# Five of eight pairs of experts: probabilities transposed in 32x32 blocks by VectorE and put in place through DRAM

## The chip, the cores and the metric

The kernel runs on one core of a Trainium2 chip. The metric is the device time of one launch in microseconds, the median of several runs. Engines are named as in the profile: PE is TensorE's matmul and PEld its weight load, DVE is VectorE, ACT is ScalarE, POOL is GpSimd, SP is SyncE, on whose queue all DMAs of this kernel are issued.

## The reference

Three stages follow one another, all in float32, for 4 batches of 448 positions: attention with 12 heads and a soft cap, a gated feed-forward stage with a short convolution, and four experts, each a causal attention of its own, of which two are kept at each position. The change lies in the last one. With `x` from the stage before it, it is:

```python
logits = x @ w_gate                      # (B, S, 4); the two largest are kept, w is their softmax
for e in range(4):
    q, k, v = x @ wq[e], x @ wk[e], x @ wv[e]          # (B, S, 64)
    scores = scale * (q @ k.transpose(0, 2, 1))
    scores = np.where(causal, -1e9, scores)
    a = softmax(scores)                                # (B, S, S)
    ye = a @ v @ wo[e]
    out += (chosen[e] * w[e]) * ye
```

The product `a @ v` sums over keys. TensorE sums over partitions, so the probabilities, which come out of the softmax with queries on the partitions, must be turned so that keys are there.

## The kernel before, in words

All four batches pass through attention first. The feed-forward results of batches 0 to 2 are made in between, left in DRAM (`g_dram`) and read back as the last stage wants them; a convolution with its gate (`conv_gate`, line 878) is done early, ahead of the store, for the first `EARLY_N[b]` of a batch's eight blocks (line 73), and after the read for the others (`prep_g`, line 1007). Then the output weights of the feed-forward stage are folded into those of the experts (`fold_mm`, line 811), and the last stage goes batch by batch.

In the last stage `v_unit` (1133) makes a batch's values and gate logits, in a tile of 4 blocks of 128 keys by 260 columns (the last block half filled), and `proj_unit` (1096) its queries and keys, 8 units of 12 matmuls a batch, which DMAs from SBUF to SBUF (`pl.move`, 1125 to 1131) then bring to the other half of the partitions, 20 for each batch. The experts go in two pairs, `i` = 0 and 1. `scores2` (1191) makes the scores of a pair in seven blocks of queries: three of 128 queries for each of the two experts, with 128, 256 and 384 keys, and one that holds the last 64 queries of both, with 448 keys. VectorE masks them and finds their maximum, ScalarE takes the exponential into SBUF, and `norm2` (1222) scales them by one over the sum and the gate's weight.

`tr2` (1241) turns them: for each expert two units of four TensorE transposes of 128x128 into a PSUM bank (banks 5 and 6 in turn, `TB`), and from there two copies, of 448 and of 64 columns, into SBUF (`PTT`, eight tiles of 512). So a pair has 16 transposes and 8 copies. `pv2` (1264) multiplies by the values, key block after key block, with the two experts side by side in the two halves of TensorE's columns, and `wo_unit` (1287), for the last batch `wo_first` and `wo_rest`, make the output, six blocks a batch.

The order of the work is a written-out list. The program makes every operation (`Plan.add`, line 238) without issuing it; `ORDER` (line 78) then says in which order the operations are issued, and so the order on each engine and on SP's queue. `SWAP` (line 178) lists the operations that go to the other of VectorE and ScalarE than the code says. `Plan.pages` (218) only serves to find out which operations depend on which. Each engine works through its own part of the list in order. The tail of the program is in the order of `TAIL` (line 193), before the list rearranges it.

Of the kernel before, what the change touches and what calls it, by code (L numbers as in the profile page):

```python
# [19 lines left out]
E = 4  # L20
# [21 lines left out]
HALF_END = 1  # L42
# [30 lines left out]
EARLY_N = (0, 4, 4, 0)  # L73
TR_E = (0, 0)
# [115 lines left out]
T_ORDER = ("q0", "q1", "tr0", "tr1", "pv0", "tr2", "tr3", "pv1", "wo")  # L190
T_LAST = ("q0", "q1")
T_REST = 12
TAIL = ("2tr0", "2tr1", "2pv0", "3q0", "2tr2", "2tr3", "3q1", "2pv1", "3tr0", "3tr1", "2wo0", "2wo1", "3pv0",
        "2wo2", "2wo3", "2wo4", "2wo5", "3tr2", "3tr3", "3woA", "3pv1", "3woB")


# [1232 lines left out]
```

## Time and profile before

| | |
|---|---|
| median of 3 runs | 530.38 us (530.14 to 531.41) |
| the profiled execution | 530.21 us |
| its span, first to last instruction | 528.5 us |
| TensorE matmul, busy | 520.6 us (99%), 3312 instructions |
| VectorE, busy | 451.8 us (85%) |
| ScalarE, busy | 364.9 us (69%) |
| DMA | 63.84 MB, mean 121 GB/s |

The profile is of one execution. Attention takes the time to about 230 us, the folding to about 362, and the last stage the rest. Busy time of TensorE includes the modelled ends of its pipelined matmuls. In groups of instructions a line is that of a helper for most operations: 380 issues matmuls, 384 transposes, 314 ScalarE's operations, 322 VectorE's, 389 DMAs. `ps` is PSUM, `fm` the float32 tile in SBUF and `rm` the one for TensorE's fast float32 format.

### The profile page before, as it was taken

How to read it: one execution, taken by the hardware profiler on the slowest of the kernel's cores; microseconds unless marked ns; L12 is line 12 of the kernel's file. 1: busy time of each engine (PE TensorE's matmuls, PEld its weight loads, DVE VectorE, ACT ScalarE, POOL GpSimd, SP SyncE). 2: the span in 40 equal slices, each digit the busy share in tenths (PEclk: the TensorE clock that was granted, in tenths of full speed). 3: DMA queues.
4: the chain of work that ended last, by engine and by line, in shares of the span. 5: the costliest groups of instructions: out<-in, count | busy, mean ns of one | idle time of the engine just before them, and what ended most of it. 6: DMA issues, size and time to landing. Idle time of an engine off the chain costs nothing.

```text
span 528.5 us, 9365 instructions
## 1 busy us (share of the span) xinstructions
PE 520.6 (99%) x3312; PEld 413.5 (78%) x3312; DVE 451.8 (85%) x1083; ACT 364.9 (69%) x659; POOL 9.8 (2%) x64
## 2 busy tenths in 40 slices
PE   9999999999999999999999999999999999999997
PEld 6445587555665855869999999999978988999886
DVE  6999999999788888899869999999978998947662
ACT  7999949999896869944224556356857884736662
POOL 4000000000000000000000002000000000000000
PEclk9999999999999999999999999999999999999999
DMA  6635534342322422244564541155334325404514
GB/s 212 194 125 191 166 134 153 122 127 73 117 92 69 131 69 87 61 142 142 180 213 147 160 138 38 53 160 145 84 95 122 92 82 154 102 9 102 141 52 158
DMA packets 42543, 63.84 MB, mean 121 GB/s; under 512 B 7424, under 2 KB 31360, under 8 KB 42496
## 3 DMA queue, kind: packets, MB, share of 16 engines
q1 hardware_dynamic: 42496, 63.24, 39.5%
q8 instruction: 26, 0.43, 0.3%
q14 instruction: 21, 0.17, 0.1%
HBM read 40.94 MB, written 12.85 MB: 102 GB/s over the span
## 4 chain that ended last, share of the span: by engine, by line
PE 90%; ACT 4%; DVE 2%; DMA 2%; SPq 1%; issue 1%
PE ps L380 87%; ACT fm L314 3%; PE ps L384 2%; DVE fm L322 1%; DVE rm L322 1%; SPq L389 1%; DMA fm<-w_in 1%; DMA fm<-kq 1%; ACT rm L314 1%; DMA rm<-rm 0%; DVE ps L322 0%
## 5 line engine op out<-in xcount | busy, mean ns | idle before, releaser
L380 PE MATMUL ps<-rm 128*128 128x448 f32 (+5 forms) x2316 | 399.4, 350 | 3.2 <-ACT fm L314 2.3
L380 PEld LDWEIGHTS ps<-rm 128*128 128x128 f32 (+1 forms) x2316 | 353.1, 187 | 47.4 <-ACT fm L314 9.8
L314 ACT ACTIVATE fm<-fm 128x448 f32<-128x448 f32 (+6 forms) x217 | 162.1, 773 | 35.8 <-DVE fm L322 21.8
L322 DVE SCALAR_TENSOR_TENSOR fm<-fm 128x448 f32<-128x448 f32 (+4 forms) x240 | 148.2, 631 | 8.6 <-ACT fm L314 5.7
L314 ACT ACTIVATE fm<-ps,fm 128x896 f32<-128x896 f32 (+5 forms) x142 | 110.0, 794 | 31.8 <-DVE fm L349 12.6
L380 PE MATMUL ps<-fm 128*64 128x448 f32 (+9 forms) x868 | 114.7, 470 | 1.7 <-DVE fm L578 1.1
L380 PEld LDWEIGHTS ps<-fm 128*64 128x64 f32 (+4 forms) x868 | 46.1, 135 | 63.1 <-issue 49.1
L322 DVE TENSOR_TENSOR rm<-fm,rm 128x448 fp32r<-128x448 f32 (+3 forms) x154 | 87.1, 583 | 4.7 <-ACT rm L314 3.2
L314 ACT ACTIVATE fm<-ps 128x448 f32<-128x448 f32 (+4 forms) x111 | 49.3, 468 | 49.6 <-PE ps L380 34.3
L322 DVE TENSOR_TENSOR fm<-fm 64x448 f32<-64x448 f32 (+6 forms) x112 | 60.9, 550 | 5.0 <-ACT fm L314 2.7
L322 DVE TENSOR_SCALAR fm<-fm 128x256 f32<-128x256 f32 (+8 forms) x143 | 43.1, 315 | 10.7 <-ACT fm L314 6.8
L314 ACT ACTIVATE rm<-fm 128x448 fp32r<-128x448 f32 (+5 forms) x77 | 39.6, 543 | 12.1 <-DVE fm L322 7.1
L314 ACT ACTIVATE rm<-ps 128x386 fp32r<-128x386 f32 (+3 forms) x46 | 19.9, 438 | 29.8 <-PE ps L380 28.7
L322 DVE COPY fm<-ps 128x448 f32<-128x448 f32 (+5 forms) x47 | 20.1, 434 | 12.6 <-PE ps L380 7.7
L322 DVE CAST rm<-fm 128x448 fp32r<-128x448 f32 (+4 forms) x85 | 29.7, 367 | 1.1 <-PE ps L380 0.3
L322 DVE TENSOR_TENSOR rm<-ps,rm 128x386 fp32r<-128x386 f32 (+1 forms) x32 | 18.7, 586 | 4.5 <-ACT rm L314 4.2
L322 DVE TENSOR_TENSOR fm<-fm,ps 128x448 f32<-128x448 f32 (+1 forms) x30 | 16.4, 568 | 5.3 <-PE ps L380 3.9
L349 DVE CUSTOM_DVE_ANT_0 ps<-ps,fm 128x256 f32<-128x256 f32 (+1 forms) x32 | 11.4, 364 | 7.0 <-PE ps L380 6.0
L384 PE MATMUL ps<-fm 128*128 128x128 f32 x128 | 17.2, 272 | 0.0
L384 PEld LDWEIGHTS ps<-fm 128*128 128x128 f32 x128 | 15.0, 140 | 1.2
L322 DVE TENSOR_REDUCE fm<-ps 128x1 f32<-128x384 f32 (+1 forms) x24 | 13.8, 576 | 0.4
L314 ACT ACTIVATION_READ_ACCUMULATOR fm<-ps,fm 128x1 f32 x56 | 11.0, 196 | 0.0
(24 smaller groups left out, 64.4 us busy)
## 6 DMA issues: line engine op xcount, KB each, us to landing
g_dram<-fm SPq DMA_DIRECT2D x32, 224.0 KB, 2.3
fm<-g_dram SPq DMA_DIRECT2D x32, 224.0 KB, 2.9
fm<-w_in SPq DMA_DIRECT2D x24, 256.0 KB, 2.7
fm<-woT SPq DMA_DIRECT2D x16, 384.0 KB, 3.3
fm<-kq SPq DMA_DIRECT2D x23, 256.0 KB, 3.3
out<-fm SPq DMA_DIRECT2D x23, 224.0 KB, 2.3
fm<-v SPq DMA_DIRECT2D x24, 192.0 KB, 2.7
fm<-kq SPq DMA_DIRECT2D x23, 192.0 KB, 3.2
```

The costliest lines, as they stand in the source:

```text
L314: return self.add("act", cost, [lambda: self.nc.scalar.activation(out, in_, func, **kw)], [out] + more, [in_] + ptr)
L322: return self.add("dve", cost, [lambda: f(out, *ins, **kw)], [out], aps)
L349: self.add("dve", cost, [lambda: self.nc.vector.tensor_tensor_reduce(x, x, mask, -1.0, 3.0e38, OP.add, OP.min, least)], [x, least], [x, mask])
L380: self.nc.tensor.matmul(out, a, b, start=start, stop=stop, **kw))
L384: calls = [lambda o=o, i=i, d=d: self.nc.tensor.transpose(o, i, d) for o, i, d in parts]
L389: self.add("dma", 470.0, [lambda: self.nc.sync.dma_start(out, in_)], outs, ins, size=size, **kw)
```

## The change

For five of the eight pairs (all but both of batch 0 and the second of batch 3, `BY_PE`) the transposes on TensorE go. The exponential writes the probabilities of a pair into one tile of 128 x 2048 columns, arranged as four parts `m` of 16 blocks of 32 columns; VectorE turns each part in place, 32x32 block by block (four instructions of 128x512). Two stores bring the tile to DRAM (`p_dram`) and four loads bring it back, so that partition 4x+m holds key 32m+x of each block of 128 keys. The values of batches 1 to 3 are put in the same order of keys by one store and one load (`spread_v`). In `pv2` a product is cut in two: the whole query blocks, and the shared block of 64 queries.

The other three pairs are turned as before, with four PSUM banks (`QB`) that they share with the scores. The shared block of scores now goes through the exponential with 512 columns, the last 64 of them at -1e30, which VectorE writes into the four banks at first and again after each turn of batch 0 (`hide_rest`). `EARLY_N` goes from 4 to 8 for batch 2. The identity for the transposes is made later, the half-filled key block lies in the lower partitions instead of the upper ones, and a branch that was not taken goes (`HALF_END`). `ORDER` and `SWAP` are new throughout; there are 2497 operations instead of 2489.

```diff
-EARLY_N = (0, 4, 4, 0)
+EARLY_N = (0, 4, 8, 0)
...
-TAIL = ("2tr0", "2tr1", "2pv0", "3q0", "2tr2", "2tr3", "3q1", "2pv1", "3tr0", "3tr1", "2wo0", "2wo1", "3pv0",
-        "2wo2", "2wo3", "2wo4", "2wo5", "3tr2", "3tr3", "3woA", "3pv1", "3woB")
+TAIL = ("2pv0", "2pv1", "3q0", "3q1", "2wo0", "2wo1", "2wo2", "2wo3", "2wo4", "2wo5", "3pv0", "3woA", "3pv1", "3woB")
+P2_AT = ((0, 1, 2), (5, 2, 1))
+BY_PE = ((0, 0), (0, 1), (3, 1))
+P2_S = 12
+P2_R = 32 * (P2_S + NT)
...
+    def hide_rest():
+
+        for t in QB.bufs:
+            x = t[:, S:]
+            pl.add("dve", 190.0, [lambda x=x: nc.vector.memset(x, -1.0e30)], [x], [])
+
-    QB, TB = Ring([bank(3), bank(4)]), Ring([bank(5), bank(6)])
+    QB = Ring([bank(i) for i in range(3, 7)])
...
-        pl.act(P2[i][k], ps[:, :n], AF.Exp, bias=mx, scale=-1.0 if fused else 1.0, accum_out=RS2[i][:, 0, k:k + 1])
+        x = ps if shared else ps[:, :n]
+        x = x if (b, i) in BY_PE else x.rearrange("p (n m x) -> p n m x", m=4, x=32)
+        pl.act(P2[i][k], x, AF.Exp, bias=mx, scale=-1.0 if fused else 1.0, accum_out=RS2[i][:, 0, k:k + 1])
...
+    def spread_v(b):
+        x, to = V2F
+        pl.store(v_dram[b], x, keys_out=[("v", b)])
+        pl.load(to, v_dram[b].rearrange("(m k) x -> k m x", m=4), keys_in=[("v", b)])
+        V2[b, "spread"] = V2T.bufs[1]
...
+    def turn(b, i):
+        if (b, i) in BY_PE:
+            return turn_by_pe(b, i)
+        t, PT[i] = P2[i][NS], PTT.next()
+        for m in range(4):
+            x = t[:, P2_R * m:P2_R * m + P2_R]
+            pl.dve("transpose", x, x)
+            if m % 2:
+                c = slice(P2_R * (m - 1), P2_R * (m + 1))
+                pl.store(p_dram[2 * b + i][:, c], t[:, c], keys_out=[("p", b, i, m // 2)])
+        for a in range(4):
+            to = PT[i][:, P2_R * a:P2_R * a + P2_R]
+            src = p_dram[2 * b + i, 32 * a:32 * a + 32].rearrange("k (m x) -> (k m) x", m=4)
+            pl.dma(to, src, sb_out=to, size=128 * P2_R * 4, keys_in=[("p", b, i, 0), ("p", b, i, 1)])
...
     def pv2(b, i):
         ps = R1 if i else bank(1)
         parts = []
+        by_pe = (b, i) in BY_PE
+        vt = V2[b] if by_pe else V2[b, "spread"]
+        u = None if by_pe else PT[i].rearrange("p (a n x) -> p n a x", a=4, x=32)
         for c in range(NT):
...
+                if c < NK:
+                    at_, sj, sc = P2_AT[h]
+                    n = at_ + (sj + sc) * c
+                    o = ps[a, 128 * c:128 * NK].rearrange("p (j a x) -> p j a x", a=4, x=32)
+                    parts.append((o, y, u[:, n:n + sj * (NK - 1 - c) + 1:sj], c == 0, False))
+            for h, (a, _) in enumerate(sides):
+                e = 2 * i + h
+                y = vt[:, c, D * e:D * e + D]
+                parts.append((cut(ps[a, 128 * NK:S], 2), y, u[:, P2_S + c, 2 * h:2 * h + 2], False, c == NK))
         pl.mm(parts)
```

`turn` is the last unit of a pair's scores; `turn_by_pe` is `tr2` for the whole pair with banks of `QB`, followed by `hide_rest` for batch 0.

The numbers in `ORDER` count the operations as the program makes them, so the last ones can be told from the end (2496): 21 of `wo_rest` (from 2476), 3 of `pv2` for pair (3,1), 5 of `wo_first`, 3 of `pv2` for (3,0) (2465 to 2467, TensorE first), 18 of batch 2's output (2447 to 2464, TensorE's every third), 12 of `turn_by_pe` for (3,1) (2435 to 2446), 10 of its `norm2`, 24 of its scores (2401 to 2424), 10 of `turn` for (3,0) (2391 to 2400: two transposes, a store, two transposes, a store, four loads), 10 of its `norm2`, 24 of its scores (2357 to 2380), 2 of `spread_v` for batch 3 (2355, 2356), and 3 each of `pv2` for (2,1) (from 2352) and (2,0) (from 2349). The stretch of the new list around that turn:

```diff
+2298 2382 2383 2384 2274 2390 2385 2272 2100 2386 2388 2387 2389 2394 2395 2335 2391 2337 2343 2344 2392 2134 2350
+2275 2352 2351 2338 2345 2346 2336 2401 2353 2354 2404 2348 2402 2407 2403 2405 2347 2406 2411 2408 2447 2412 2330
+2332 2135 2409 2410 2414 2453 2415 2396 2334 2413 2417 2418 2393 2448 2356 2419 2421 2422 2423 2454 2416 2131 2399
+2450 2456 2451 2459 2397 2420 2424 2400 2425 2462 2426 2398 2427 2434 2431 2430 2429 2449 2428 2432 2433 2438 2455
+2444 2445 2435 2439 2457 2436 2441 2442 2446 2440 2463 2443 2465 2437 2473 2452 2474 2466 2467 2472 2470 2468 2471
```

## Rows read from the trace of the kernel before

**Rows 1.** The page, part 1: busy us (share of the span) and count of each engine.

```profile
PE 520.6 (99%) x3312; PEld 413.5 (78%) x3312; DVE 451.8 (85%) x1083; ACT 364.9 (69%) x659; POOL 9.8 (2%) x64
```

**Rows 2.** Stretches: length, busy us of PE, PEld, DVE, ACT, POOL, clock, DMA share, GB/s.

```profile
0.00:57.00 57.00, 52.95 (x396) 28.58 (x396) 51.44 (x129) 52.97 (x59) 5.92 (x51) 1.00 0.54 173
57.00:362.00 305.00, 305.00 (x1890) 239.36 (x1891) 273.14 (x545) 205.32 (x308) 3.62 (x11) 1.00 0.39 121
362.00:528.00 166.00, 162.64 (x1030) 145.57 (x1028) 127.17 (x412) 106.61 (x294) 0.22 (x2) 1.00 0.37 103
```

**Rows 3.** The waits of TensorE's matmuls: us in total, times, longest.

```profile
PE ps L380 <- ACT fm L314: 2.8, 6, 0.9
PE ps L380 <- DVE fm L578: 1.1, 1, 1.1
```

**Rows 4.** The chain of waits by line, then in time: start, us, what.

```profile
by line: PE ps L380 87.5%; ACT fm L314 3.2%; PE ps L384 2.3%; DVE fm L322 1.3%; DVE rm L322 1.0%; SPq L389 0.9%; issue 0.8%; DMA fm<-w_in 0.7%; DMA fm<-kq 0.6%; ACT rm L314 0.5%; DMA rm<-rm 0.5%; DVE ps L322 0.1%
...
56.96 317.03 PE ps L380 x1972
374.00 0.87 PE ps L384 x8
...
424.50 0.44 PE ps L384 x4
424.94 2.45 PE ps L380 x12
...
497.98 2.38 DMA rm<-rm
...
500.41 0.73 PE ps L380 x4
```

**Rows 5.** TensorE's groups by shape, whole run: busy us, mean ns.

```profile
L384 PE MATMUL ps<-fm 128*128 128x128 f32 x128 | 17.2, 272 | 0.0
...
L380 PE MATMUL ps<-fm 128*64 128x64 f32 x32 | 2.3, 220 | 0.0
```

**Rows 6.** TensorE in time: two pairs' products with the values (start, us, what).

```profile
388.91 3.68 PE L380 MATMUL ps<-fm 128*64 128x448 f32 x32
```

**Rows 7.** VectorE's and ScalarE's groups by shape, whole run: busy us, mean ns.

```profile
L322 DVE SCALAR_TENSOR_TENSOR fm<-fm 128x448 f32<-128x448 f32 x128 | 81.7, 649 | 5.5 <-ACT fm L314 4.2
...
L314 ACT ACTIVATE fm<-ps 128x448 f32<-128x448 f32 x80 | 42.2, 541 | 37.9 <-PE ps L380 25.2 <-DVE fm L322 7.1 <-PE ps L384 4.5
...
L322 DVE SCALAR_TENSOR_TENSOR fm<-fm 128x896 f32<-128x896 f32 x24 | 27.5, 1146 | 1.5 <-ACT fm L314 1.5
...
L322 DVE TENSOR_SCALAR fm<-fm 128x448 f32<-128x448 f32 x13 | 5.8, 449 | 2.6 <-ACT fm L314 1.9 <-DMA fm<-g_dram 0.7
...
L314 ACT ACTIVATE fm<-ps 128x64 f32<-128x64 f32 x16 | 3.5, 220 | 0.0
...
L322 DVE COPY fm<-ps 128x64 f32<-128x64 f32 x16 | 3.4, 217 | 2.1 <-ACT fm L314 2.1
```

**Rows 8.** SP's queue in time: start, us, what it issues.

```profile
448.17 33.69 SPq L389 DMA_DIRECT2D rm<-rm  x20
...
499.25 0.46 SPq L389 DMA_DIRECT2D rm<-rm  x1
```

**Rows 9.** SP's own waits: us in total, times, longest.

```profile
SPq L389 <- DVE fm L322: 166.7, 61, 9.2
```

**Rows 10.** DMA: queue 1 (packets, MB, share); issues: KB each, us to landing.

```profile
q1 hardware_dynamic: 42496, 63.24, 39.5%
...
g_dram<-fm SPq DMA_DIRECT2D x32, 224.0 KB, 2.3
fm<-g_dram SPq DMA_DIRECT2D x32, 224.0 KB, 2.9
fm<-w_in SPq DMA_DIRECT2D x24, 256.0 KB, 2.7
...
fm<-wo SPq DMA_DIRECT2D x2, 384.0 KB, 3.8
```

More of the change, by code (lines that the diff above doesn't have):

```diff
@@ L41 @@
 MERGE = ()
-HALF_END = 1
 P_3 = 10
@@ L72 @@
 PR_L = 110.0
-EARLY_N = (0, 4, 4, 0)
-TR_E = (0, 0)
+EARLY_N = (0, 4, 8, 0)
 V_N = (4, 2, 2, 2)
@@ L229, in pages @@
                 runs = [(lo, hi + step * (n - 1)) for lo, hi in runs]
-        halves = {min(p // 64, 1) for p in (first, first + dims[0][1] - 1)}
+        quarters = range(first // 32, (first + dims[0][1] - 1) // 32 + 1)
         for lo, hi in runs:
@@ L234, in pages @@
                 whole = lo <= page * self.PAGE and hi >= (page + 1) * self.PAGE
-                for h in halves:
-                    yield (ap.tensor.name, h, page), whole and dims[0][1] >= 64
+                for h in quarters:
+                    yield (ap.tensor.name, h, page), whole and dims[0][1] >= 32
     def add(self, eng, cost, calls, outs, ins, keys_out=(), keys_in=(), size=0, modes=None):
@@ L471, in chain_kernel @@
     g_dram = tc.dram_tile([B, 128, NF, S], F32, name="g_dram")
+    v_dram = tc.dram_tile([B, 128, NT * NV], F32, name="v_dram")
+    p_dram = tc.dram_tile([2 * B, 128, 4 * P2_R], F32, name="p_dram")
     def at(pos, kind=None):
@@ L496, in decode @@
         pl.stt(m.bitcast(I32), lo, 29, c, OP.logical_shift_right, OP.bitwise_or)
-    ident, one_0, low_row = fm.take(128), fm.take(96), fm.take(1)
+    ident_at = fm.at
+    one_0, low_row = fm.take(96), fm.take(1)
     cw = fm.take(NF * 3)
@@ L591, in chain_kernel @@
     at(-50)
-    pl.add("pool", 500.0, [lambda: make_identity(nc, ident)], [ident], [])
     one_r = [cut(t, 3) for t in (one_0, one_1)]
@@ L974, in chain_kernel @@
     OTT = fm.ring(3, S)
-    V2T = Ring([cut(t, NT) for t in fm.ring(2, NT * NV).bufs])
+    V2F = fm.ring(2, NT * NV).bufs
+    V2T = Ring([cut(t, NT) for t in V2F])
     gt, ge = (fm.take(NT * E * E, gate_at + n).rearrange("p (k a b) -> p k a b", k=NT, a=E) for n in (0, 64))
@@ L983, in chain_kernel @@
     MXT = fm.ring(4, 1)
-    P2T = fm.ring(2, 2 * 768 + S)
-    PTT = fm.ring(8, 512)
+    P2T, PTT = fm.ring(2, 4 * P2_R), fm.ring(2, 4 * P2_R)
     GX, VS = cut(fm.take(NF * KR), NF), fm.take(NV)
@@ L1072, in chain_kernel @@
             base=0, channel_multiplier=0)
+    ident = fm.take(128, ident_at)
     def late_loads(pos):
         at(pos)
+        pl.add("pool", 500.0, [lambda: make_identity(nc, ident)], [ident], [])
         for t in QZT.bufs + QLT.bufs:
             for a, c in ((lo64, slice(SG - 64, SG)), (hi64, slice(SG - 128, SG - 64))):
-                pl.act(t[a, c], ident[a, :64], AF.Copy, scale=0.0)
+                pl.act(t[a, c], tri[a, :64], AF.Copy, scale=0.0)
         for t in QPT.bufs:
@@ L1082, in late_loads @@
         for t in V2T.bufs:
-            pl.pool("memset", t[:64, NK, :E * D], 0.0, cost=400.0)
-        pl.pool("memset", VS[:64, :E * D], 0.0, cost=400.0)
+            pl.pool("memset", t[64:, NK, :E * D], 0.0, cost=400.0)
+        pl.pool("memset", VS[64:, :E * D], 0.0, cost=400.0)
         for i in range(2):
@@ L1135, in v_unit @@
         if t == 0 and not part:
-            V2[b] = V2T.next()
+            V2[b] = V2T.bufs[not b]
         if not part:
@@ L1154, in v_unit @@
             for x, a in both:
-                pl.pick(0, x[64:], ps[a, :NV])
+                pl.pick(0, x[:64], ps[a, :NV])
             for x, a in both:
-                pl.pick(1, x[:64, E * D:], ps[a, E * D:NV])
+                pl.pick(1, x[64:, E * D:], ps[a, E * D:NV])
     def gate(b):
@@ L1211, in scores2 @@
             t = P2T.next()
-            at_ = [0, 128, 384, 768, 896, 1152, 1536, 1536 + S]
-            P2[i] = [t[:, at_[x]:at_[x + 1]] for x in range(NS)]
+            u = t.rearrange("p (m n x) -> p n m x", m=4, x=32)
+            at_ = [0, 128, 384, 768, 896, 1152, 1536, 4 * P2_R]
+            P2[i] = [t[:, at_[x]:at_[x + 1]] for x in range(NS)] if (b, i) in BY_PE else [u[:, at_ + sj * x:at_ + sj * x + sc * x + 1:sc] for at_, sj, sc in P2_AT for x in range(NK)]
+            P2[i] += [t] if (b, i) in BY_PE else [u[:, P2_S:], t]
             RS2[i] = RST.next()
@@ L1239, in chain_kernel @@
     TR_SH = ((0, 1), (3, 2))
-    def tr2(b, e, k):
-        i, h = divmod(e, 2)
-        if not h and not k:
-            for x in range(2):
-                PT[2 * i + x] = [PTT.next(), PTT.next()]
-        ps = TB.next()
-        at_, sh, to = TR_AT[h][k]
-        parts = []
-        for (c, j), n in zip(TR_C[k], at_):
-            parts.append((ps[:, n:n + 128], P2[i][NK * h + j][:, 128 * c:128 * c + 128], ident))
-        c = TR_SH[h][k]
-        kk = slice(128 * c, 128 * c + 128) if c < NK else slice(S - 128, S)
-        out = ps[:, sh[0]:sh[0] + 128]
-        if sh[1] - sh[0] != 64:
-            n = min(sh[0], 128)
-            out = cut(ps[:, n:n + 384], 2)[:, :, sh[0] - n:sh[0] - n + 64]
-        parts.append((out, P2[i][NS - 1][:, kk], ident))
-        pl.transposes(parts)
-        own = slice(64 * h, 64 * h + S)
-        either(TR_E[k], PT[e][k][:, :S], ps[:, own])
-        other = sh[1 - h]
-        either(TR_E[1 - k], PT[e ^ 1][k][:, to:to + 64], ps[:, other:other + 64])
+    def spread_v(b):
[3 more added lines that the diff above has]
+        V2[b, "spread"] = V2T.bufs[1]
@@ new lines, in turn_by_pe @@
+    def turn_by_pe(b, i):
+        t = PTT.next()
+        PT[i] = [[t[:, 1024 * h + 512 * k:1024 * h + 512 * k + 512] for k in range(2)] for h in range(2)]
+        for h in range(2):
+            for k in range(2):
+                ps = QB.next()
+                at_, sh, to = TR_AT[h][k]
+                parts = []
+                for (c, j), n in zip(TR_C[k], at_):
+                    parts.append((ps[:, n:n + 128], P2[i][NK * h + j][:, 128 * c:128 * c + 128], ident))
+                c = TR_SH[h][k]
+                out = ps[:, sh[0]:sh[0] + 128]
+                if sh[1] - sh[0] != 64:
+                    n = min(sh[0], 128)
+                    out = cut(ps[:, n:n + 384], 2)[:, :, sh[0] - n:sh[0] - n + 64]
+                parts.append((out, P2[i][NS - 1][:, 128 * c:128 * c + 128], ident))
+                pl.transposes(parts)
+                own = slice(64 * h, 64 * h + S)
+                either(0, PT[i][h][k][:, :S], ps[:, own])
+                other = sh[1 - h]
+                either(0, PT[i][1 - h][k][:, to:to + 64], ps[:, other:other + 64])
+        if (b, i) != (B - 1, 1):
+            hide_rest()
@@ L1266, in pv2 @@
         parts = []
+        by_pe = (b, i) in BY_PE
+        vt = V2[b] if by_pe else V2[b, "spread"]
+        u = None if by_pe else PT[i].rearrange("p (a n x) -> p n a x", a=4, x=32)
         for c in range(NT):
+            if by_pe:
+                for h, (a, _) in enumerate(sides):
+                    e = 2 * i + h
+                    rhs = PT[i][h][c in (1, 2)][:, PT_C[h][c]]
+                    parts.append((ps[a, 128 * c:S], vt[:, c, D * e:D * e + D], rhs, c == 0, c == NK))
+                continue
             for h, (a, _) in enumerate(sides):
                 e = 2 * i + h
-                rhs = PT[e][c in (1, 2)][:, PT_C[h][c]]
-                parts.append((ps[a, 128 * c:S], V2[b][:, c, D * e:D * e + D], rhs, c == 0, c == NK))
+                y = vt[:, c, D * e:D * e + D]
[4 more added lines that the diff above has]
+                    parts.append((o, y, u[:, n:n + sj * (NK - 1 - c) + 1:sj], c == 0, False))
+            for h, (a, _) in enumerate(sides):
+                e = 2 * i + h
+                y = vt[:, c, D * e:D * e + D]
+                parts.append((cut(ps[a, 128 * NK:S], 2), y, u[:, P2_S + c, 2 * h:2 * h + 2], False, c == NK))
         pl.mm(parts)
@@ L1303, in wo_rest @@
                 pl.mm(wo_parts(b, m, wop[m], (1,)))
-            elif not HALF_END:
-                wop.append(TB.next())
-                pl.mm(wo_parts(b, m, wop[m], (0, 1)))
             else:
@@ L1310, in wo_rest @@
                 for k in range(2):
-                    c, ps, ot = slice(n * k, n * k + n), TB.next()[:, :n], PTT.next()[:, :n]
+                    c, ps, ot = slice(n * k, n * k + n), QB.next()[:, :n], GT.next()[:, :n]
                     pl.mm([(ps, x, y[:, c], *z) for _, x, y, *z in wo_parts(b, m, ps, (0, 1))])
@@ L1315, in wo_rest @@
                 continue
-            wo_out(b, m, wop[m], PTT.next()[:, :S])
+            wo_out(b, m, wop[m], GT.next())
     def unit(cost, f, *args, lag=0.0):
@@ L1335, in t_parts @@
         for i in range(2):
-            parts[f"q{i}"] = [unit(0.3, scores2, b, i, k) for k in range(NS)] + [unit(0.0, norm2, b, i)]
+            parts[f"q{i}"] = [unit(0.3, scores2, b, i, k) for k in range(NS)] + [unit(0.0, norm2, b, i), unit(0.5, turn, b, i)]
             parts[f"pv{i}"] = [unit(1.9, pv2, b, i)]
-        for e in range(E):
-            parts[f"tr{e}"] = [unit(0.5, tr2, b, e, k) for k in range(2)]
         return parts
@@ L1355, in chain_kernel @@
             late_loads(pos)
+            hide_rest()
         pos = merge(proj_units(b), with_prep(b + 1, t), pos)
+        if b:
+            at(pos, "spread%d" % b)
+            spread_v(b)
     b = B - 1
@@ L1361, in chain_kernel @@
         p, k = (t3 if n[0] == "3" else t2), n[1:]
+        if n == "3q0":
+            at(pos, "spread%d" % b)
+            spread_v(b)
         if k in p:
```

2 lines of the change are left out of this document (1 added, 1 removed), and 211 rows, old and new, of tables (ORDER, SWAP).

## The prediction

> **What bounds the kernel now.** I read the page's summary first. TensorE is busy for 520.6 of 528.5 us [rows 1]. Then the stretches: the granted clock is 1.00 in each, so the upper of its two levels; between 57 and 362 us TensorE is busy for 305.00 of 305 us, and between 362 us and the end for 162.64 of 166; VectorE is at 273.14/305 = 90% and 127.17/166 = 77% there, ScalarE lower, the DMA engines at 0.39 and 0.37 [rows 2]. The two longest waits of TensorE's matmuls sum to 3.9 us [rows 3], and the chain of waits runs through TensorE for 317 us without a break [rows 4]. So nothing hides TensorE's work: an instruction less there is time less, as long as what replaces it is never waited for.
>
> **What leaves TensorE.** A pair of experts has 16 transposes (two experts, two units, four each); 8 pairs make the 128 of the trace [rows 5]. The chain shows 8 of them in 0.87 us and 4 in 0.44, so 0.109 us each, with the matmul behind them at its usual pace (12 in 2.45 us) [rows 4]: switching costs nothing beside them. The same line holds 2.3% of the chain, 12.2 us for the 112 transposes on it, again 0.109. Five of eight pairs go: 80 x 0.109 = **8.7 us less**. The other end is the group's busy time, 17.2 x 5/8 = 10.8 us [rows 5], but its ends are modelled and overlap the next instruction; I keep 8.7.
>
> **What comes onto TensorE.** The products with the values had 448 + 320 + 192 + 64 = 1024 columns for each expert; now they have 384 + 256 + 128 and four pieces of 64, 1024 again. Two pairs take 32 instructions in 3.68 us [rows 6]: each float32 product runs as two instructions, with two experts side by side. There are three more products an expert, so 3 x 2 x 5 = 30 more such side-by-side instructions. If only columns count they cost 0. At most each costs what the 64-column form shows, 2.3 us / 16 = 0.144, less its columns' 0.058 (64 of the 4096 columns in 3.68 us), or 0.086 x 30 = 2.6 us [rows 5, 6]; but that again is mostly a modelled end. A gain is excluded, the columns being the same. Nearest is the dense run itself, whose 16 steps follow one another without an idle time in the view, so near the lower end: an eighth of the way, **0.35 us more**.
>
> **VectorE.** It gets 20 transposes of 128x512, an operation that the trace doesn't show. From below it is at the pace of the scalar operation, 0.449 us for 448 columns, so about 0.5; from above 1.15 us, an operation of 896 columns. The one-pass float32 operations take 0.649 us for 448 columns and 1.146 for 896, so 0.72 for 512 [rows 7]; a transpose is one such pass, so I take that: 14.4 us. The 12 memsets of 64 PSUM columns, at the 0.217 us of a 64-column copy out of PSUM, add 2.6. Gone are 20 copies of 448 columns out of PSUM (0.541 us, mostly ScalarE) and 20 of 64 (0.22, half on each engine): 13 us of ScalarE, 2.2 of VectorE [rows 7]. Four conv gates of batch 2 move from after 362 us to before it (EARLY_N 4 to 8), each four three-operand instructions of 0.649 on VectorE: 10.4 us. So after 362 us VectorE has 127 + 14.8 - 10.4 = 131 of about 158 us, 83%; before, 273 + 10.4 = 284 of 305, 93%. It stays below TensorE in both, and all of this is hidden under TensorE at nothing; without that cover it would cost up to the 14.8 us of its sum. The wider shared block (512 columns for 448) adds 64 x 0.84 ns = 0.05 us to each of eight exponentials, hidden too. The later identity, the moved padding and the branch that goes fall to POOL, 2% busy [rows 1], or to nobody: nothing. The finer pages of the planner issue no instruction.
>
> **DMA and its queue.** Five pairs bring 2 stores of 512 KB and 4 loads of 256 KB each, three batches one store and one load of 520 KB: 36 transfers, 13.7 MB. All go on SP's queue, at 0.46 us an issue [rows 8], 17 us of a queue that waited 166.7 us for one VectorE line alone [rows 9]. Queue 1 moved 63.24 MB in 39.5% of the span, so 303 GB/s when busy [rows 10]; 13.7 MB is 45 us, and the last stretch goes from 0.37 to about 0.64. Hidden, as long as nobody waits for a landing.
>
> **The tightest place** is pair (3,0), in the tail. Counted in the new list, the operations of TensorE between the last VectorE transpose (2392) and that pair's product with the values (2465) are the product of pair (2,1), 3.68/2 = 1.84 us [rows 6]; fifteen score matmuls of pair (3,1), 4416 columns, 2.0; 36 output matmuls of batch 2 at 0.204, 7.35; sixteen transposes, 1.74 [rows 4]: 12.9 us of cover. The round trip under it: four transposes 2.9; a 512 KB store, from 2.3 (224 KB) to 4.5 (the loads' 2.9 at 224 KB and 3.8 at 384 KB, extended), taken at 3.4; five issues in front of the last load, 1.9; its landing, 2.7 to 3.8, taken at 3.0 [rows 8, 10]. Together 11.2, at best 8.9 (transposes of 0.5 us) and at worst 14.8 (of 1.15): a slack of 1.7, or a wait of 1.9 us. For the other four pairs a batch's projections (8 units of 12 matmuls at 0.204, 20 us) stand in between. For new waits in all I take 0.8 us, between 0 and 1.9.
>
> The Trainium skill, "DMA: Bandwidth & Descriptors", section "Anatomy of one DMA — SWDGE (gpsimd) path", gives 2.0 us and bytes over 436 GB/s for another issue path: 3.2 us for the store, 2.6 for the load. The trace agrees about the fixed part (2.3 and 2.9 us for 224 KB), so by it nothing would be waited for, and the sum would be 0.8 us less, 522.0.
>
> **Sum.** The profiled execution took 530.21 us, of which 528.5 is its span: 530.21 - 8.7 + 0.35 + 0.8 = 522.65. The median of the runs is 0.17 above that execution: **522.8 us**.
>
> **The rivals.**
> *Part is given back.* The new order leaves TensorE waiting for landings at two or three places (the product of pair (2,1), the values of batch 3, pair (3,0)). Each late landing costs at most 2.3 to 2.9 us [rows 10]; one to two of them beside the above give 525 to 528.5. For it: the short waits [rows 3] belong to the old order, and the list is wholly new. Against it: the cover counted above.
> *No gain.* What leaves TensorE comes back as waits, because the transpose through VectorE takes 11 us from end to end where TensorE takes 16 x 0.109 = 1.7; 1.7 us uncovered in each of five pairs is 8.4, and the time 531. The Trainium skill says so in "VectorE: DVE Perf Modes", section "Rules for kernel authors": a 128x128 transpose belongs on TensorE where its result may go to PSUM, VectorE turning blocks of 32x32 only. The trace speaks for it only in that the copies out of PSUM were nearly free here; against it, TensorE is the one engine that is full [rows 2].
> *Slower: SP's queue.* It issues in order. A load that waits for its pair's store holds every transfer behind it for the store's landing, about 3.4 us. Behind it stand the moves that put queries and keys of the next batch in place: 20 of them between 448 and 482 us, and at 497.98 one for which TensorE's next matmul waited [rows 4, 8]. Six holds (four pairs, two V reorders) fall among those moves. With no slack, three cost 10.2 us: 530.4 - 8.35 + 10.2 = 532.3. It decides from 10 us of holds that reach TensorE. Against it: the queue is mostly idle, and the moves come in bursts.
> *More.* Only the first 57 us leave TensorE idle, for 4.05 us [rows 2]. If the new list wins that back too, the time is 518.6.
>
> **How the numbers follow.** A measurement of this kernel can tell about 0.3% from no change, 1.6 us: faster is below 528.8, slower above 532.0. Chances: gain kept (520.5 to 524.5) 0.62; part given back 0.16; more 0.06; no gain 0.07; slower 0.09. Faster sums to 0.84. The range goes from 518.5, the first stage's idle time won back (the 10.8 us of the other end would give 520.5, inside it), to 529, where the second case ends; it leaves out the last two cases and half of "more", 0.19.
>
> **What would show it.** Right: 48 transposes on TensorE at 0.109 us, 20 on VectorE near 0.72 us, TensorE still busy for 305 us of the middle, its matmuls' waits below 6 us in all, ScalarE some 13 us shorter. Wrong: waits of TensorE for DMA of the turned tiles or for the moves, VectorE transposes above 1.5 us, idle stretches of TensorE between 180 and 362 us behind conv gates, or matmuls of 64 columns that take more than 0.1 us each pair.

## The result, and the profile after

The changed kernel takes 524.45 us (median of 4 runs, 523.81 to 526.76) against 530.79 for the kernel before on the same chip: a ratio of 0.989 (95% interval 0.9855 to 0.9922), 6.3 us less. A second set of runs on another chip gave 525.3 against 530.65, 0.990 (0.9887 to 0.9915). The forecast was 522.8, in a range of 518.5 to 529.0: inside the range, 1.7 us below the result. The profiled execution took 524.19 us, 6.0 less than that of before.

First the page's line of engines, part 1, then the stretches (length, busy us of PE, PEld, DVE, ACT, POOL, clock, DMA share, GB/s), both of the kernel after; they answer to [rows 1, 2].

```profile
PE 511.1 (98%) x3292; PEld 405.8 (78%) x3292; DVE 451.6 (86%) x1075; ACT 366.2 (70%) x659; POOL 9.3 (2%) x64
```

```profile
57.00:362.00 305.00, 305.00 (x1894) 239.19 (x1891) 275.56 (x547) 218.85 (x336) 4.04 (x15) 1.00 0.39 119
362.00:522.00 160.00, 153.78 (x1010) 138.95 (x1008) 124.70 (x399) 94.55 (x269) 0.00 (x0) 1.00 0.63 193
...
400.00:440.00 40.00, 38.77 (x274) 35.70 (x273) 37.25 (x100) 30.83 (x81) 0.00 (x0) 1.00 0.76 237
...
480.00:500.00 20.00, 18.80 (x137) 15.89 (x136) 14.94 (x55) 10.61 (x34) 0.00 (x0) 1.00 0.90 282
```

The last stage is shorter, but TensorE, idle there for 166 - 162.64 = 3.4 us before, is now idle for 6.2; 2.6 and 2.7 us of these lie behind its last matmul. VectorE reads 124.70 of 160, 78%, as an average; the third line is the stretch that matters, 37.25 of 40 us, 93%, with the DMA engines at 0.76. The waits of TensorE's matmuls in the kernel after (us in total, times, longest) show where the idle time is; they answer to [rows 3]:

```profile
PE ps L381 <- ACT fm L315: 3.8, 7, 1.1
PE ps L381 <- DVE fm L582: 1.1, 1, 1.1
PE ps L381 <- DMA fm<-p_dram: 0.9, 1, 0.9
PE ps L381 <- DVE rm L323: 0.8, 1, 0.8
PE ps L381 <- DMA rm<-rm: 0.7, 2, 0.4
PE ps L381 <- ACT rm L315: 0.6, 1, 0.6
```

They sum to 7.9 us; the same view of before summed to 4.3 (the two rows of [rows 3] and one of 0.4). From 362 us on it is 3.3 for 0.4; the 0.8 for VectorE's line 323 is new too, but lies in the first 57 us. Two are new in kind: the turned probabilities' loads, and the moves. TensorE in time shows them (start, us, what, and in brackets the idle time before it). The second line is the product of pair (1,1) with the values, held 0.93 us; the third, held 0.30, is TensorE's next work behind it.

```profile
432.06 1.98 PE L381 MATMUL ps<-fm 128*64 128x384 f32 x28
434.97 1.98 PE L381 MATMUL ps<-fm 128*64 128x384 f32 x28 [0.93 <-DMA fm<-p_dram]
437.25 4.09 PE L381 MATMUL ps<-rm 128*128 128x256 f32 x21 [0.30 <-DMA rm<-rm]
...
507.96 3.71 PE L381 MATMUL ps<-fm 128*64 128x384 f32 x44
```

The groups by shape of the kernel after (busy us, mean ns) show the operations that stayed and those that came, and its DMA view (KB each, us to landing) the transfers:

```profile
L323 DVE STREAM_TRANSPOSE fm<-fm 128x512 f32<-128x512 f32 x20 | 13.2, 692 | 0.2
...
L385 PE MATMUL ps<-fm 128*128 128x128 f32 x48 | 5.7, 272 | 0.0
...
L1197 DVE MEMSET ps<- 128x64 f32 x12 | 1.2, 112 | 0.2
```

```profile
q1 hardware_dynamic: 47680, 76.92, 47.5%
...
p_dram<-fm SPq DMA_DIRECT2D x10, 512.0 KB, 3.5
fm<-p_dram SPq DMA_DIRECT2D x20, 256.0 KB, 4.3
...
rm<-rm SPq DMA_DIRECT2D x32, 128.0 KB, 3.0
```

The loads land in 4.3 us. The moves, untouched by the change, land in 3.0 us; in the run without the new transfers, below, the same row says 2.3.

### The profile page after: what moved, and what is told of

Read it like the earlier page. It is cut to its first block, busy times and chain, and to the rows that moved or that the text cites. A ratio compares the mean times of both kernels' runs of the same rounds, so it can differ in the third digit from the quotient of the medians.

```text
span 522.5 us, 9375 instructions
## 1 busy us (share of the span) xinstructions
PE 511.1 (98%) x3292; PEld 405.8 (78%) x3292; DVE 451.6 (86%) x1075; ACT 366.2 (70%) x659; POOL 9.3 (2%) x64
## 4 chain that ended last, share of the span: by engine, by line
PE 91%; DVE 2%; DMA 2%; ACT 2%; SPq 1%; issue 1%; ACTq 0%
PE ps L381 90%; ACT fm L315 2%; DVE fm L323 1%; DMA rm<-rm 1%; SPq L390 1%; PE ps L385 1%; DVE rm L323 1%; DMA fm<-kq 1%; ACT rm L315 0%; ACTq L315 0%
## 5 line engine op out<-in xcount | busy, mean ns | idle before, releaser
L315 ACT ACTIVATE fm<-fm 128x448 f32<-128x448 f32 (+7 forms) x231 | 167.2, 758 | 42.5 <-DVE fm L323 32.9
L315 ACT ACTIVATE fm<-ps,fm 128x896 f32<-128x896 f32 (+4 forms) x142 | 110.2, 795 | 27.5 <-DVE fm L323 12.9
L381 PE MATMUL ps<-fm 128*64 128x448 f32 (+10 forms) x928 | 114.8, 450 | 2.9 <-DVE fm L582 1.1
L323 DVE TENSOR_TENSOR rm<-fm,rm 128x448 fp32r<-128x448 f32 (+4 forms) x154 | 86.6, 584 | 3.4 <-ACT rm L315 2.3
L315 ACT ACTIVATE fm<-ps 128x448 f32<-128x448 f32 (+5 forms) x87 | 39.4, 471 | 36.1 <-PE ps L381 26.5
L315 ACT ACTIVATE rm<-fm 128x448 fp32r<-128x448 f32 (+4 forms) x83 | 43.3, 546 | 18.3 <-DVE fm L323 14.1
L323 DVE TENSOR_SCALAR fm<-fm 128x256 int32<-128x256 int32 (+12 forms) x129 | 38.5, 313 | 6.0 <-DMA fm<-g_dram 1.6
L323 DVE CAST rm<-fm 128x384 fp32r<-128x384 f32 (+5 forms) x79 | 27.4, 360 | 1.2 <-DMA fm<-kq 0.8
L323 DVE COPY fm<-ps 128x448 f32<-128x448 f32 (+4 forms) x32 | 16.0, 512 | 14.0 <-PE ps L381 12.0
L323 DVE STREAM_TRANSPOSE fm<-fm 128x512 f32<-128x512 f32 x20 | 13.2, 692 | 0.2
```

The lines of the kernel that those rows point to most:

```text
L315: return self.add("act", cost, [lambda: self.nc.scalar.activation(out, in_, func, **kw)], [out] + more, [in_] + ptr)
L323: return self.add("dve", cost, [lambda: f(out, *ins, **kw)], [out], aps)
L381: self.nc.tensor.matmul(out, a, b, start=start, stop=stop, **kw))
```

## The experiments

**The change once more**, with no edit, beside the three runs on record with it.

> The changed kernel itself, beside the three others: the time to compare them with. 524.4 us again by every theory (523.8 to 525).

525.3 us (524.55 to 526.0), the 0.990 given above; this is what the next runs on the kernel after are held against. The later ones come from other chips, where the kernel before took 530.58 to 530.82.

**What the transposes on TensorE were worth.** Four runs. The first adds 16 transposes ahead of each of the five changed products, 80 in all, to the kernel after.

```diff
         pl.mm(parts)
+        if not by_pe:
+            pl.ops[-1].calls[:0] = [lambda: nc.tensor.transpose(ps[:, :128], ident, ident)] * 16
```

> The changed kernel, with 16 transposes of the identity put on TensorE ahead of each of the five new products with the values (their result is overwritten). Theory (TensorE is full, so each of its instructions is paid): 80 x 0.109 = 8.7 us more than the changed kernel, 533.1 us (532 to 534). Rival (the last stage is now set by waits, of which TensorE's idle time there shows 3.5 us): these 3.5 us take up part of it, 529 to 530.

It took 530.42 us, a ratio of 0.9995 (0.9986 to 1.0004) to before: 5.1 us more than the change beside it (525.3), not 8.7; neither figure came, the rival's is the nearer. With the transposes back, the new order takes as long as the old. TensorE's waits for the turned probabilities are gone from its view and their sum falls to 5.5 us: part of the added work lies where TensorE waited.

The second takes the 80 transposes out of the kernel before and leaves everything else, its order too.

```diff
         pl.transposes(parts)
+        if (b, i) not in ((0, 0), (0, 1), (3, 1)):
+            pl.ops[-1].calls.clear()
```

> The kernel before, in its old order, with the 80 TensorE transposes of the same five pairs left out and the copies out of PSUM kept (the five pairs compute other values). Theory (the whole gain is TensorE's time): 530.8 - 8.7 = 522.1 us (521.5 to 522.8), which is 2.3 less than the changed kernel. Rival (the gain of the changed kernel comes from the new list and the earlier conv gates, and the transposes were partly hidden): 526 or more.

It took 527.37 us, 0.9939 (0.9926 to 0.9953): only 3.3 us of the 8.7, and the rival's figure. The third also leaves out the 40 copies out of PSUM that follow these transposes.

```diff
         either(TR_E[k], PT[e][k][:, :S], ps[:, own])
+        if (b, i) not in ((0, 0), (0, 1), (3, 1)):
+            pl.ops[-1].calls.clear()
         other = sh[1 - h]
         either(TR_E[1 - k], PT[e ^ 1][k][:, to:to + 64], ps[:, other:other + 64])
+        if (b, i) not in ((0, 0), (0, 1), (3, 1)):
+            pl.ops[-1].calls.clear()
```

> The kernel before without the 80 TensorE transposes of the five pairs and also without their 40 copies out of PSUM (13 us of ScalarE, about 2 of VectorE; the five pairs compute other values). Leaving out the transposes alone gave 527.4. First theory (the copies, in ScalarE's order, are what TensorE then waits for): 530.65 - 8.7 = 522 us. Second theory (VectorE at 37 of 40 us, and the softmax that TensorE now reaches earlier): 527.4, no more gained; in between, 524 to 526, if both.

526.11 us, 0.9912 (0.9899 to 0.9925): another 1.3 us, so the copies are a part of what is missing, but a small one. In TensorE's timeline of this run three waits for ScalarE are left behind 480 us, 1.85 us in all:

```profile
484.09 8.16 PE L380 MATMUL ps<-rm 128*128 128x384 f32 x41 [0.71 <-ACT fm L314]
...
497.77 1.83 PE L380 MATMUL ps<-rm 128*128 128x384 f32 x8 [0.91 <-ACT fm L314]
499.83 5.73 PE L380 MATMUL ps<-rm 128*128 128x128 f32 x27 [0.23 <-ACT fm L314]
```

The fourth run starts again from the second, with the copies in, and makes room on VectorE and ScalarE: it also leaves out the steps of the last batch's convolution gates.

```diff
+        for o in pl.ops:
+            if str(o.kind).startswith("prep_g3") and o.eng != "dma":
+                o.calls.clear()
         pl.issue()
```

> The kernel before without the 80 transposes (527.4 us) and, on top, without the 36 VectorE and 28 ScalarE steps of the last batch's convolution gates (22 us and 15 us of work after 362 us): the last batch's gates are left out, its transposes are left out. Theory: after 362 us the two engines beside TensorE are as full as TensorE, and that is why leaving the transposes out gave 3.3 us and not 8.7; with room on both the rest comes back: 522 us. Rival: it is chains in the order of the steps (a softmax's row sums, a copy that frees a bank), which stay as long when the engines are emptier: 526 us or more.

525.63 us, 0.9907 (0.9893 to 0.992): 1.7 us by the medians, 2.3 by the spans of the two profiled executions, between the theory's 522 and the rival's 526, near the rival, and the stretches say why. First two of the kernel before, then three of the kernel without the transposes, then three without the gates too:

```profile
400.00:440.00 40.00, 39.95 (x269) 36.26 (x268) 37.13 (x109) 30.17 (x79) 0.00 (x0) 1.00 0.36 98
...
480.00:500.00 20.00, 20.00 (x128) 17.24 (x128) 15.45 (x64) 13.85 (x42) 0.00 (x0) 1.00 0.46 122
```

```profile
400.00:440.00 40.00, 38.38 (x243) 34.06 (x242) 37.69 (x112) 30.71 (x82) 0.00 (x0) 1.00 0.38 105
440.00:480.00 40.00, 39.51 (x232) 37.17 (x232) 28.64 (x93) 21.53 (x58) 0.00 (x0) 1.00 0.35 89
480.00:500.00 20.00, 17.58 (x104) 14.35 (x103) 15.55 (x66) 15.02 (x47) 0.00 (x0) 1.00 0.47 130
```

```profile
400.00:440.00 40.00, 39.77 (x250) 35.57 (x251) 27.17 (x93) 21.46 (x62) 0.00 (x0) 1.00 0.39 109
440.00:480.00 40.00, 40.00 (x236) 37.75 (x235) 21.43 (x80) 18.25 (x53) 0.00 (x0) 1.00 0.36 91
480.00:500.00 20.00, 17.36 (x102) 13.85 (x101) 15.12 (x65) 15.48 (x49) 0.00 (x0) 1.00 0.41 116
```

Between 400 and 440 us VectorE was already 93% busy before the change. Without the transposes TensorE arrives early and waits there; with 10 us less work on VectorE and 9 on ScalarE in the stretch it is full again (38.38 to 39.77, then 40.00). That is the theory of two full engines, for some 2 us; the run leaves out work and the order's steps together, so which of the two engines it was stays open. Between 480 and 500 us this theory fails: TensorE loses 2.4 us of 20 without its transposes and gets none of it back when the gates go. TensorE's timeline of the kernel without the transposes names what it waits for:

```profile
485.20 8.14 PE L380 MATMUL ps<-rm 128*128 128x384 f32 x41 [1.36 <-ACT fm L314]
...
495.62 1.95 PE L380 MATMUL ps<-fm 128*64 128x448 f32 x16 [0.40 <-ACT fm L314]
...
498.88 1.83 PE L380 MATMUL ps<-rm 128*128 128x384 f32 x8 [0.65 <-ACT fm L314]
500.95 3.31 PE L380 MATMUL ps<-rm 128*128 128x128 f32 x15 [0.24 <-ACT fm L314]
```

Four waits for ScalarE, 2.65 us, and without the gates the same four sum to 2.64; without the copies, which ScalarE mostly makes, 1.85 are left. Neither engine is full there (15 of 20 us). Before, 31 transposes stood in these 20 us, 3.4 us at 0.109. My reading, which no run tries alone, is that they filled the time while the scores and softmax of the last batch went from engine to engine. So in the old order, by this reading, about 2.3 us of the 8.7 were hidden by full engines between 400 and 480 us, and 2.65 by such a chain after 480. With the 2.9 us by which the span fell that is 7.9; 0.8 stays unassigned.

**What the replacement costs.** The kernel after without the 30 transfers of the probabilities, whose products then use stale values:

```diff
                 pl.store(p_dram[2 * b + i][:, c], t[:, c], keys_out=[("p", b, i, m // 2)])
+                pl.ops[-1].calls.clear()
...
             pl.dma(to, src, sb_out=to, size=128 * P2_R * 4, keys_in=[("p", b, i, 0), ("p", b, i, 1)])
+            pl.ops[-1].calls.clear()
```

> The changed kernel without the 30 transfers that bring the turned probabilities through DRAM (the products read what batch 0 left in the tile, so the five pairs compute other values; VectorE's transposes stay). Theory (what was given back are waits for landings, its own and those of the moves beside them: four waits, 1.8 us): 524.4 - 1.8 = 522.6 us, and the moves land in 2.3 us again instead of 3.0. Rival (the new list has ScalarE late in two places, 1.7 us, and landings cost nothing): 524.4, the same as the changed kernel. Second rival (every wait of the last stage hangs on the transfers): 524.4 - 3.5 = 520.9.

523.28 us, 0.987 (0.9851 to 0.9889): 2.0 us less than the change beside it, about the 1.8 of the theory. The share of the DMA engines between 400 and 440 us falls from 0.76 to 0.49, and the moves land in

```profile
rm<-rm SPq DMA_DIRECT2D x32, 128.0 KB, 2.3
```

But TensorE's waits from 362 us on only fall from 3.3 to 2.8 us, and 2.1 of these are now for the moves. So the 2.0 us are the price of the transfers as a whole, with their issues and traffic; the run doesn't give the price of the late landings alone.

Then the same without VectorE's 20 transposes too:

```diff
             pl.dve("transpose", x, x)
+            pl.ops[-1].calls.clear()
```

> The changed kernel without the 30 transfers and without the 20 VectorE transposes (the five pairs compute other values). Leaving out the transfers alone gave 523.3. First theory (VectorE's 13.2 us are hidden): 523.3 again. Second theory (VectorE shares the bound of the last stage): 1 to 3 us less, 520.5 to 522.5, with TensorE's waits for ScalarE and VectorE shorter.

522.74 us, 0.9844 (0.9831 to 0.9856): 0.5 us less again by the medians, 1.4 by the two ratios, whose intervals just overlap. It lies between the two theories (523.3, and 520.5 to 522.5), so VectorE's 13.2 us cost some 0.5 to 1.4 us, hardly clear of the scatter. It is also a floor: with nothing in place of TensorE's 80 transposes the new order gives 522.7, and what is left are waits for the moves (2.6 us), ScalarE (2.4) and VectorE (2.5), of which 3.2 lie after 362 us. How much more VectorE could take was asked by running ten of the transposes three times over:

```diff
             pl.dve("transpose", x, x)
             if m % 2:
+                pl.ops[-1].calls *= 3
+            if m % 2:
```

> The changed kernel with two of the four VectorE transposes of each pair done three times (the same values): 20 more, 20 x 0.692 = 13.8 us of VectorE. First theory (VectorE is hidden under TensorE at nothing): 525.0 us, as the changed kernel. Second theory (VectorE and TensorE are both full where pairs (1,0) and (1,1) are turned: VectorE is busy for 37.25 of the 40 us from 400 on, so 5.5 us more find 2.8 us of idle time): 3 to 9 us more, 528 to 534.

534.91 us, 1.0071 (1.0044 to 1.0097): 9.6 us more than the change for 13.8 us of VectorE, just beyond the second theory's 528 to 534. It is not one number for VectorE: the first 13 us are nearly hidden, the next 14 are not. They also lengthen each round trip by up to 2.8 us, and TensorE's clock falls behind the waits, so the run doesn't tell load from delay and clock. Its waits, and a stretch right behind the longest (length, PE, PEld, DVE, ACT, POOL, clock):

```profile
PE ps L381 <- DMA fm<-p_dram: 4.9, 3, 2.9
```

```profile
437.00:439.00 2.00, 1.77 (x10) 1.06 (x12) 0.79 (x3) 1.10 (x2) 0.00 (x0) 0.50 1.06 405
```

The granted clock is 0.50 there, the lower level, where the kernel after has 1.00 from 400 to 500 us.

**Where the loads stand.** One load of 1 MB in place of four, issued where the first of the four stood, and then where the last stood:

```diff
+        loads = []
...
+            loads.append(pl.ops[-1])
+        whole = PT[i].rearrange("p (a x) -> p a x", a=4)
+        back = p_dram[2 * b + i].rearrange("(a k) (m x) -> (k m) a x", a=4, m=4)
...
+        loads.sort(key=lambda o: place[o.n])
+        for o in loads[1:]:
+            o.calls.clear()
+        loads[0].calls[:] = [lambda: nc.sync.dma_start(whole, back)]
```

and for the last place

```diff
-        for o in loads[1:]:
+        for o in loads[:3]:
             o.calls.clear()
-        loads[0].calls[:] = [lambda: nc.sync.dma_start(whole, back)]
+        loads[3].calls[:] = [lambda: nc.sync.dma_start(whole, back)]
```

> The changed kernel with one load of 1 MB for a pair in place of four of 256 KB, issued where the first of them was; 15 issues of 0.45 us fewer on SP's queue. First theory (the round trip and the moves behind it are late by the queue's issues): the wait for the probabilities of 0.9 to 1.3 us goes and the moves come 1.3 us earlier, so 1 to 2 us less, 523 to 524. Rival (the DMA engines are what is full, with a share of 0.76 to 0.90 there, and a landing waits for the bytes): 525, the same as the changed kernel.

> As the run with one load of 1 MB for four of 256 KB, but the one load is issued at the place of the last of the four instead of the first. Theory (the size counts: 1 MB lands in 8 us and all of it is waited for): 530 us or more again, rather later than the 530.7 us of that run, since it starts later. Rival (the place counts: issued first in line it held SyncE's queue, and with it the moves and loads behind it, until both stores had landed): 526 to 528 us.

530.72 us, 0.9996 (0.9976 to 1.0016), and 531.54, 1.0006 (0.998 to 1.0031). Neither figure of the first run's theories came (523 to 525); the second run's first theory did (530 or more): one load is 5 to 6 us slower than four, in either place. But the place was hardly tried where it counts: the four loads of pair (1,1) stand together in the list, and the two runs issue its one load at 428.69 and 428.24 us. The DMA views of the two runs:

```profile
fm<-p_dram SPq DMA_DIRECT2D x5, 1024.0 KB, 8.2
```

```profile
fm<-p_dram SPq DMA_DIRECT2D x5, 1024.0 KB, 7.8
```

Pair (1,1)'s load takes longer still, 9.6 us in the first run and 9.4 in the second, about 437.6 us there; the last of the change's four landed at 434.79, 7.1 us behind the first one's issue. TensorE in the second run, and the clock behind the second wait (length, PE, PEld, DVE, ACT, POOL, clock):

```profile
DMA to landing us min/median/max: 9.4/9.4/9.4
```

```profile
437.77 3.32 PE L381 MATMUL ps<-fm 128*64 128x384 f32 x28 [3.76 <-DMA fm<-p_dram]
...
498.80 2.93 PE L381 MATMUL ps<-fm 128*64 128x384 f32 x28 [2.57 <-DMA fm<-p_dram]
```

```profile
500.00:502.00 2.00, 2.00 (x22) 1.75 (x18) 0.00 (x0) 0.24 (x1) 0.00 (x0) 0.50 1.05 422
```

TensorE's waits sum to 11.6 us for the change's 7.9, and the two products behind them took 3.32 and 2.93 us for 1.98, at a granted clock of 0.50 over part of them. That is 3.7 + 2.3 = 6.0 us, and the profiled execution (530.05) took 5.9 more than the change's (524.19). So more than a third of the loss is the clock's. Why one load of 1 MB lands later than four was not tried.

Then a try at a better version: VectorE's transposes of pairs (1,0) and (1,1) ahead of the gate steps that stand among them, by the order alone. VectorE's part of the list, and SP's:

```diff
-1910 1951 2032 2033 2034 1952 2002 1949 1945 2003 1948 2038 2005 2043 2042 2045 2046 1972
+1951 2032 2033 2034 1952 1949 1948 2038 2043 2042 2045 2046 1910 2002 1945 2003 2005 1972
...
-1970 1953 1950 2120 2044 2047 1957 1954 1956 1955 2075 2051 2050 2049 2048
+1953 1950 2044 2047 1970 1957 1954 1956 1955 2120 2075 2051 2050 2049 2048
```

> Only the order is edited: fourteen steps of the last batch's gates (VectorE and ScalarE) and two of their loads are issued after VectorE's eight transposes of pairs (1,0) and (1,1) instead of among them, so that the stores of these pairs start about 2.7 us earlier (five gate steps of 0.55 to 0.68 us on VectorE). Theory: the landing of these pairs' loads is what TensorE waits for at 433.8 us (0.93 us), so the kernel takes 524.3 us, some 0.9 us less than the change, against 530.8 before. Rival: VectorE is full there in any order and what is put off comes late in its turn (the gates' own readers, the moves at 436.7 us): 525 us or more.

531.22 us, 1.0014 (1.0003 to 1.0026): 6 us slower than the change. The rival's "525 us or more" covers it, but not by its reason. SP's queue of this run in time (start, us, what), TensorE in time, and a stretch of it:

```profile
417.33 5.38 SPq L396 DMA_DIRECT2D p_dram<-fm  x4
...
423.32 2.32 SPq L396 DMA_DIRECT2D fm<-p_dram  x4
427.50 4.87 SPq L396 DMA_DIRECT2D fm<-g_dram  x2
432.42 1.85 SPq L396 DMA_DIRECT2D fm<-p_dram  x4
```

```profile
432.18 1.98 PE L387 MATMUL ps<-fm 128*64 128x384 f32 x28
440.01 3.31 PE L387 MATMUL ps<-fm 128*64 128x384 f32 x28 [5.85 <-DMA rm<-rm]
```

```profile
441.00:442.00 1.00, 1.00 (x10) 0.53 (x8) 0.30 (x2) 0.00 (x0) 0.00 (x0) 0.50 0.68 138
```

Two gate loads (`fm<-g_dram`) now stand ahead of pair (1,1)'s loads. The second needs a buffer that the postponed gates free only at 432 us, and holds the queue until then: the loads go out at 432.42, where the change issues them at 427.67. TensorE stands for 5.85 us, and when it goes on the clock is 0.50 and 28 instructions that take 1.98 us take 3.31. The view names the moves, but the last of the loads, issued at 433.85, lands after 6.0 us, at 439.85, and TensorE starts at 440.01: by these times it was the load. The landing of the last two loads:

```profile
DMA to landing us min/median/max: 5.5/5.7/6.0
```

The last run puts fewer steps off, so that the queue isn't held:

```diff
-1910 1951 2032 2033 2034 1952 2002 1949 1945 2003 1948 2038 2005 2043 2042 2045 2046 1972
+1910 1951 2032 2033 2034 1952 1949 1948 2038 2043 2042 2045 2046 2002 2003 1945 1972 2005
...
-1970 1953 1950 2120 2044 2047 1957 1954 1956 1955 2075 2051 2050 2049 2048
+1970 1953 1950 2044 2047 1957 1954 1956 1955 2120 2075 2051 2050 2049 2048
```

> Only the order is edited, less than in the run that was 6 us slower: four gate steps of VectorE (2.3 us) and three of ScalarE go behind the transposes of pairs (1,0) and (1,1), one gate load behind the loads of pair (1,0), and the gate that it feeds behind the projection's steps; the second gate load, whose wait of 4.5 us held the loads of pair (1,1) and the moves on SyncE's queue in that run, finds its buffer free as in the change. Theory (that run lost its time to the held queue, not to the transposes' place): the 6 us are gone, the wait of 0.93 us for the landing at 433.8 us is shorter or gone, 524.3 us, and no more than 525.3. Rival (gates that are put off and bunched up cost by themselves, whatever the queue does): 527 us or more.

526.48 us, 0.9921 (0.9903 to 0.994): most of the 6 us is back, which was the theory's main point, but not the 0.9 that it hoped for. It lies between the theory's 525.3 and the rival's 527, 1.2 us above the change's 525.3, with overlapping intervals. TensorE in time with the clock behind its wait, SP's queue ahead of pair (1,1)'s loads, and the landing of the last two of them:

```profile
437.63 1.98 PE L387 MATMUL ps<-fm 128*64 128x384 f32 x28 [3.56 <-DMA rm<-rm]
```

```profile
437.00:442.00 5.00, 4.37 (x42) 3.85 (x43) 2.79 (x13) 1.22 (x5) 0.00 (x0) 1.00 0.42 125
```

```profile
425.55 2.72 SPq L396 DMA_DIRECT2D fm<-g_dram  x2
428.37 1.81 SPq L396 DMA_DIRECT2D fm<-p_dram  x4
```

```profile
DMA to landing us min/median/max: 6.7/7.2/7.7
```

The landing of the last one in the kernel after:

```profile
DMA to landing us min/median/max: 5.8/5.8/5.8
```

The last load went out at 429.75 and landed at 437.45; in the change, 428.99 and 434.79, with TensorE on its way 0.18 us later in both. The turned tiles are stored 1 us earlier than in the change and still come back 2.7 us later. Two gate loads go out in the 3 us ahead of them, where the change has one; that these slow them is likely, but it wasn't tried alone. What ends the wait at 434 us is the last landing of pair (1,1), and it did not come earlier with VectorE's transposes. Here, behind a wait of 3.56 us, the clock stayed at 1.00. No version that computes the whole result came out faster than the change.

## Why the prediction came out as it did

**The premise fell.** "An instruction less there is time less" was read from TensorE's 162.64 of 166 us [rows 2]. The 8.7 us were sized rightly: in the kernel after the chain gives 16 transposes 1.75 us, 0.109 each. But taken alone out of the old order they gave 3.3 us, and put back into the new one they cost 5.1. An engine that is 99% busy can owe part of its work to time in which it would otherwise wait. The old order gave 4.7 with the copies gone too. With nothing in place of the transposes (only the values still go through DRAM) the kernel after takes 522.74 against 530.82 beside it, 8.1 of the 8.7: the 3.4 us beyond 4.7 come with the rest of the change (the new lists, the four gates moved ahead, the four banks), which no run takes apart. Of the 8.1 the replacement takes 2.6 back (525.3).

**VectorE at nothing: nearly right, for a wrong reason.** Its transposes took 0.692 us (0.72 taken), the memsets 0.112 (0.217 taken), and cost 0.5 to 1.4 us, hardly clear of the scatter. But the average of 83% hid a stretch of 93%, and the next 14 us, with the longer round trips and the lower clock that came with them, cost 9.6. ScalarE did not get 13 us shorter: 364.9 before, 366.2 now, and VectorE did not get longer (451.8 and 451.6), which fits a new list of swaps that gives work of VectorE to ScalarE; it was not taken apart. I had counted the operations and not the lists that place them.

**The products with the values.** 0.35 us was taken; 44 instructions, one pair of each kind, take 3.71 us where two pairs of the old kind took 3.68 [rows 6]: 0.03 a pair, 0.15 in all.

**New waits: the term that was mis-sized.** 0.8 us was taken; TensorE's waits rose by 3.6, most of it after 362 us, where they went from 0.4 to 3.3. Of these 3.3 the view gives 0.9 to the loads themselves, 0.7 to the moves and 1.7 to ScalarE, for which the sum had no term. The step that failed for the loads is their landing, 3.0 us taken from a stage with less traffic [rows 10], 4.3 measured with the DMA share at 0.76 (0.64 was foreseen for the whole stretch, and 0.63 came). The place was wrong too: pair (3,0), the tightest by my count, waited for nothing of its own; pair (1,1), for which I saw 20 us of projections in between, waited 0.93. The count for (3,0) had a slip besides: five issues at its own 0.46 us are 2.3, not 1.9. Of the signs set out beforehand, the waits below 6 us (7.9) and the shorter ScalarE did not come, and one sign of being wrong did: waits for the turned tiles and the moves, 1.6 us.

The Trainium skill's line for a DMA ("DMA: Bandwidth & Descriptors", section "Anatomy of one DMA — SWDGE (gpsimd) path") is for another issue path; worked out from it, 2.6 us for such a load and no wait was an estimate. The trace shows 4.3 in this stage, and the measurement decides.

**The number.** By the profiled executions: -8.7, +0.15 and +3.6 make -5.0, and -6.0 came; 1.0 us is unassigned, about the scatter between runs. That the forecast is 1.7 us off, no more, is in part luck: it priced the transposes at 8.7 us where the old order gives 3.3 to 4.7, and waits that it didn't foresee stand against a gain of the new order that it didn't foresee either.

**The rivals.** "Part is given back" (525 to 528.5) has its mechanism in the trace, at the lower end of its price (524.45, and 525.3 in the second set). "No gain" wanted 8.4 us of waits in the five pairs; the replacement takes 2.6 back in all. By the Trainium skill ("VectorE: DVE Perf Modes", section "Rules for kernel authors") the transposes should have stayed on TensorE. Here, with TensorE full, the change that moves five pairs' of them gave 6 us, and the measurement decides. "Slower: SP's queue" did not come: SP waited 2.5 us in all for the stores to `p_dram`. But the edit of the order that put one more gate load ahead of four loads gave a loss of that kind, 531.22, by a load that was held for its buffer and not for a store.

**Left open.** Of the floor's 8.1 us, how much is the new order's alone was not separated, nor what the late landings cost without the rest of the transfers; loads on another queue than SP's were not tried.

## What to carry to other kernels

Before an operation on the fullest engine is priced at its duration, leave it out of the kernel as it stands: what comes back is the price in that order, and the stretch by stretch busy shares of the other engines (93% here under an average of 77%) give a first hint of what hides the rest. A round trip through DRAM is priced by its last landing with the traffic of that stretch. Here four loads came back sooner than one of the same bytes. Look also at what stands ahead of its loads on the queue. Where one queue issues everything, a load that waits for a buffer stops all that is behind it, so a change of order on one engine must be read on the queue too.

## What the runs showed that was not expected

A long wait of TensorE can cost more than itself. After 5.85 us without work, the granted clock was 0.50 (1.2 of 2.4 GHz) in the next two microseconds, and 28 matmuls took 3.31 us for 1.98; in the run with more VectorE transposes it was 0.50 for the two us shown, behind waits of 2.9 us and less. With the one load issued last, it fell to 0.50 behind waits of 3.76 and 2.57 us. After 3.56 us in the last run it stayed at 1.00, so the length of one wait alone doesn't tell. And a transfer's landing time is not its own: the untouched 128 KB moves went from 2.3 to 3.0 us, and the last 256 KB load of pair (1,1) landed in 5.8 and in 7.7 us, with other transfers around it.
